# Pool makes a token tile's second norm as soon as its statistics are there, and more key tiles go to P·V as f16 products

## The chip, the cores and the metric

The kernel runs on one core of a Trainium2 chip. The metric is device time in microseconds (us): the median over executions of the program. The engines are named as in the profile: PE is the matrix engine (PEld its weight loads), DVE the vector engine, ACT the scalar engine, POOL the GpSimd engine, SP the engine whose queue issues most DMAs. Each engine works off its own instructions in the order in which the program wrote them; an instruction that waits for data holds up everything behind it on its engine.

## The reference

One transformer block with modulated layer norms: 2048 tokens, width 512, 32 query heads of 16 that share one key head and one value head, and a bilinear GLU of width 1792. Cut to what is computed:

```python
mod = (silu(c) @ w_mod).reshape(1, 6, 1, -1)
sa, ca, ga, sb, cb, gb = (mod[:, i] for i in range(6))
h = layernorm(x) * (1 + ca) + sa
q = (h @ wq).reshape(B, S, 32, 16).transpose(0, 2, 1, 3)
p = softmax(einsum("bhqd,bkd->bhqk", q, h @ wk) * 16 ** -0.5)
o = einsum("bhqk,bkd->bhqd", p, h @ wv)
x = x + ga * (o.transpose(0, 2, 1, 3).reshape(B, S, 512) @ wo)
h = layernorm(x) * (1 + cb) + sb
x = x + gb * (((h @ w_gate) * (h @ w_up)) @ w_down)
```

## The kernel before

**Units, blocks and turns.** The attention runs in 32 units (numbered 0 to 31). Four units in a row, with the same 256 queries and eight heads each, make a block; "a block's second unit" is unit 1, 5, 9, 13, 17, 21, 25 or 29. A unit goes over 16 key tiles of 128 keys, one in each turn, so there are 512 turns. In a turn PE makes four score tiles of 128 keys x 512 (`sc`), ACT makes their exponentials P (L690), PE finds running maxima for the unit after next (`mx`, L611, which DVE reduces, L615), and at the turn's end PE multiplies the exponentials of the turn before by the values (`pv`, L724), summed over the unit's key tiles in one PSUM bank. In the places between, PE does half matmuls of the side work (L520): the query projection, the output projection `wo` of the last block, gate and up (`wg`, `wu`), and down (`wd`). The order is written out by hand; nothing moves an instruction at run time.

Turns go in pairs: in the pair's first turn the exponentials of one row half are made for both key tiles, in the second those of the other half. So an even key tile's P is whole in the middle of the next turn, an odd one's at the end of its own.

**P·V in f32 and in f16.** Most key tiles go into P·V as f32: four matmuls with a 32-column output each (eight in the trace, as one f32 product shows as two). For a few key tiles, listed in `F16_AT` by the unit's place in its block and from unit `F16_FROM` on, P is written to one of two sets of places, Pool splits each of its four parts j = 0 to 3 into a high and a low f16 half (`p_split`, two instructions each, L696 and L697, both seen as `glu<-glu`), and PE makes three f16 products of four matmuls: high times value-high, high times value-low, low times value-high. The low halves are needed by the last four matmuls alone.

```python
def p_split(v, j):
    t, h = p_sets[f16_set[v]]
    nc.gpsimd.tensor_scalar(h[:, j, 0], t[:, j], 1.0, 0.0, op0=OP.mult, op1=OP.add)
    nc.gpsimd.tensor_tensor(h[:, j, 1], t[:, j], h[:, j, 0], op=OP.subtract)
```

An f16 tile's products are late by one f16 tile: they stand in the P·V place of the next f16 tile (`pv_place`), which is at the end of the turn behind that tile's own. The four splits are written into Pool's order in the middle of turns `f16_split`: before, in the four turns after the tile's, except for the first tile of a block's second unit, whose splits stand in its turns 1, 1, 9 and 10 (`F16_LATE`).

**The rest of Pool's order.** In the same queue stand: the second half of the GLU product, two instructions per group of gate and up (L929, L930), which wait for DVE's `gf`; `mult` of `normalise` (L765, L767, L768: the unit's attention output times the reciprocal sums, `M` below), at the end of turn 10 of the next unit; and the norm of the token tiles. After a block, `wo_work(sb)` adds the output projection for the block's two tiles of 128 tokens. At a tile's end DVE adds it to x; by timers that count half turns, DVE makes the statistics (3 and 4 half turns later, `spread` and `aggr`), and six small Pool instructions make the reciprocal deviation (L221 to L226). `nrm` then makes the norm: subtract and scale (L829 on Pool in blocks 2 to 5; elsewhere ACT, L831, which needs two more small Pool instructions, L823 and L824, for its bias), times and plus the modulation (L835, L836), and two f16 halves (L838, L839). Before, both tiles' norms wait for the second tile: they are written 4 and 9 half turns after its end. In blocks 1 to 6 (`by_dma`) a DMA transposes the result, and two half turns after that gate and up may start. Blocks are numbered from 0; all this falls in the second unit of the next block (block 3 in unit 17, block 6 in unit 29).

Of the kernel before, what the change touches and what calls it, by code (L numbers as in the profile page):

```python
# [25 lines left out]
NC = KC  # L26
NU = NS * NC
KT = S // 128
# [20 lines left out]
M_STEP = 23  # L49
PAIRED = 14  # L50
Q_BURSTS = {26: 3, 27: 3, 28: 3, 29: 3}
F16_FROM = 9
F16_AT = ((0, 5, 10), (0, 10), (0, 5, 10), (0, 5, 10))
F16_LATE = {0: (1, 1, 9, 10)}
P_SHIFT = float(14 * np.log(2.0))

LOW = -3.0e38
# [12 lines left out]
def adaln_mqa_glu_kernel(ctx: ExitStack, tc: tile.TileContext, x_in, wq_in, wk_in, wv_in, wo_in,  # L70
# [82 lines left out]
    for i in range(3):  # L153
        t = consts.tile([128, 2, 2, ST], F16, name=f"sst{i}")
# [73 lines left out]
    def rstd_of(st, n):  # L228
        y = work.tile([128, 4], F32, name="ry", bufs=6)[:, :n]
        rstd_into(y, st[:, :, 1], n)  # L230
        return y
# [155 lines left out]
    nc.gpsimd.memset(tok, 0.0)  # L387
    kts16 = sorted({k for ks in F16_AT for k in ks})
    v16 = consts.tile([128, 2, len(kts16), 32], F16, name="v16")
# [266 lines left out]
    pd = {}  # L656
    f16s = [KT * u + k for u in range(F16_FROM, NU) for k in F16_AT[u % NC]]
    assert f16s[0] % KT == 0
    f16_set = {v: i % 2 for i, v in enumerate(f16s)}
    f16_before = dict(zip(f16s[1:], f16s))  # L660
    f16_split = {}
    for v in f16s:
        late = v % KT == 0 and v // KT % NC == 1
        for j in range(4):
            f16_split.setdefault(v + (F16_LATE[0][j] if late else j + 1), []).append((v, j))
    p_sets = []
    did_pv = {}

# [108 lines left out]
    def after(delay, f):  # L777
        if tick[0] is None:
            f()
        else:  # L780
            timers.setdefault(tick[0] + delay, []).append(f)
# [5 lines left out]
    def load_x(t):  # L787
        if t < KT - 2:
            x1s[t] = work.tile([128, D], F32, name="x1", tag="x1", bufs=6)
        else:  # L790
            x1s[t] = work.tile([128, D], F32, name="x1p", tag="P", bufs=8)
        nc.sync.dma_start(x1s[t], x_rows[t * 128:(t + 1) * 128, :])

    def wo_work(sb):
        on_pool = 2 <= sb < NS - 2
        by_dma = 0 < sb < NS - 1

        def op(t):
            def f(i):
                ch, term = divmod(i, 3)  # L800
                ol, wl = TERMS[term]
                return [(och[sb, ch][:, ol, t * 128:(t + 1) * 128], wo[:, wl, ch, :])]
            return f

        def fin(t):
            row = 2 * sb + t

            def f(p):
                x1 = x1s[row]
                nc.vector.scalar_tensor_tensor(x1, p, sca[:, 7:8], x1, op0=OP.mult, op1=OP.add)  # L810
                s2 = work.tile([128, 1, 2], F32, name="st2", bufs=5)
                bs = work.tile([128, 6], F32, name="bs", bufs=4)
                nb = work.tile([128, 2], F32, name="nb", bufs=4)
                yt = {}

                def spread():
                    nc.vector.bn_stats(bs, x1)

                def aggr():
                    nc.vector.bn_aggr(s2[:, 0, :], bs)  # L820
                    yt["y"] = rstd_of(s2, 1)
                    if not on_pool:
                        nc.gpsimd.tensor_tensor(nb[:, 0:1], s2[:, 0, 0:1], yt["y"], op=OP.mult)  # L823
                        nc.gpsimd.tensor_scalar(nb[:, 1:2], nb[:, 0:1], -1.0, 0.0, op0=OP.mult, op1=OP.add)  # L824

                def nrm():
                    n2 = work.tile([128, D], F32, name="n2", tag="n2", bufs=2)
                    if on_pool:
                        nc.gpsimd.tensor_scalar(n2, x1, s2[:, 0, 0:1], yt["y"], op0=OP.subtract, op1=OP.mult)  # L829
                    else:  # L830
                        nc.scalar.activation(n2, x1, AF.Identity, bias=nb[:, 1:2], scale=yt["y"])  # L831
                    n2s[row] = n2
                    if not by_dma:
                        return
                    nc.gpsimd.tensor_tensor(n2, n2, cbb, op=OP.mult)  # L835
                    nc.gpsimd.tensor_tensor(n2, n2, sbb, op=OP.add)  # L836
                    n16 = work.tile([128, 2, D], F16, name="n16", tag="gf", bufs=4)
                    nc.gpsimd.tensor_scalar(n16[:, 0, :], n2, 1.0, 0.0, op0=OP.mult, op1=OP.add)  # L838
                    nc.gpsimd.tensor_tensor(n16[:, 1, :], n2, n16[:, 0, :], op=OP.subtract)  # L839
                    after(TR_LAG + (3 if sb < 2 else 0), lambda: ln2_turn(sb, t, n16))  # L840

                after(3, spread)
                after(4, aggr)
                n2f[row] = nrm
                if t == 1:
                    late = 3 if sb < 2 else 0
                    for j in range(2):
                        after((4, 9)[j] + late, n2f[2 * sb + j])
                    if sb == 0:
                        after(TR_WAIT + late, lambda: turns.extend(ln2_work(sb)))  # L850
            return f

        return [Group(3 * KC, op(t), fin(t), lambda t=t: load_x(2 * sb + t)) for t in range(2)]
# [6 lines left out]
    def ln2_turn(sb, t, n16):  # L860
        to = h2s[sb].rearrange("p l k n -> p (l k) n")[:, :, t * 128:(t + 1) * 128]
        nc.sync.dma_start(to, n16.rearrange("p l d -> p (l d)"), transpose=True)
        if t == 1:
            after(H2_LAG, lambda: h2done.add(sb))

    def ln2_work(sb):
        st = {}

        def tr(i):
            def f():  # L870
                if not h2s:
                    h2T = big.tile([128, 2, 2, KC, ST], F16, name="h2T", tag="wq")
                    both = big.tile([128, 2 * KC * S], F16, name="glu", tag="big")
                    n = 2 * FT * ST
                    glus.append(both[:, :n].rearrange("p (h f t) -> p h f t", h=2, f=FT))
                    p_places(both[:, n:])
                    h2s.update({s: h2T[:, s % 2] for s in range(NS)})
                st["p"] = ps_hold("mx")
                for k in range(2):
                    for t in range(2):  # L880
                        c = k * ST + t * 128
                        nc.tensor.transpose(st["p"][:, c:c + 128],
                                            n2s[2 * sb + t][:, (2 * i + k) * 128:(2 * i + k + 1) * 128], ident)
            return f

        def ev(i):
            def f():
                hf = work.tile([128, 2, ST], F32, name="hf", tag="g", bufs=2)
                for k in range(2):
                    nc.scalar.activation(hf[:, k, :], st["p"][:, k * ST:(k + 1) * ST], AF.Identity,  # L890
                                         bias=hsc[:, 2 * i + k, 0:1], scale=hsc[:, 2 * i + k, 1:2])
                ps_give(st["p"])
                eng = nc.vector if sb == NS - 1 else nc.gpsimd
                h = h2s[sb][:, :, 2 * i:2 * i + 2, :]
                eng.tensor_scalar(h[:, 0], hf, 1.0, 0.0, op0=OP.mult, op1=OP.add)  # L895
                eng.tensor_tensor(h[:, 1], hf, h[:, 0], op=OP.subtract)
                if i == 1:
                    (after if sb == 0 else lambda d, f: f())(3, lambda: h2done.add(sb))
            return f

        return [(900, tr(i), ev(i)) for i in range(2)]
# [386 lines left out]
    nrm = []  # L1288
# [149 lines left out]
    nrm = normalise(NU - 1)  # L1438
# [34 lines left out]
```

## Time and profile before

| | us |
|---|---|
| median of 3 runs | 1674.84 (1674.62 to 1675.54) |
| profiled execution, its own time | 1674.18 |
| its span in the trace | 1672.3 |
| PE busy | 1629.1 (97%) |
| DVE busy | 1401.4 (84%) |
| ACT busy | 1221.9 (73%) |
| POOL busy | 1004.5 (60%) |

The profile's page gives the busy time of each engine, the chain of work that ended last, and groups of instructions with mean durations and the idle time ahead of them. Below are also used: the waits of one engine by what ended them, the timeline of one engine (start, duration, instruction, and in brackets the idle time before it with what ended it), and windows, which give busy time and PE's granted clock (1.00 is full speed) between two moments. In the trace one turn takes about 2.85 us and one unit about 45.5 us.

### The profile page before, as it was taken

What the parts mean: (1) busy time and instruction counts of PE and PEld (TensorE: products, weight loads), DVE (VectorE), ACT (ScalarE), POOL (GpSimd) and SP (SyncE); (2) the same over time, 40 slices, a digit from 0 to 9 for tenths busy, and PEclk for the clock granted to TensorE, in tenths of its full rate; (3) what the DMA queues carried; (4) which work ended last, traced back from release to release, by engine and by line L of the source; (5) the groups of instructions that cost most, each with busy time, mean ns of one, the idle gap of its engine ahead of it and who ended that gap; (6) DMA issues with size and microseconds to landing.
All of it is one profiled execution on the core that took longest, in us unless ns stands there. A gap on an engine that the chain in (4) does not pass through costs nothing.

```text
span 1672.3 us, 41157 instructions
## 1 busy us (share of the span) xinstructions
PE 1629.1 (97%) x15881; PEld 752.0 (45%) x15881; DVE 1401.4 (84%) x2433; ACT 1221.9 (73%) x2428; POOL 1004.5 (60%) x1372
## 2 busy tenths in 40 slices
PE   9999999999999999999998999899998999999999
PEld 4333333355433554345532454434544345454776
DVE  8999999899998999999997999799997999890211
ACT  6688888888777887778876787677876777687310
POOL 6856637875847665756656565754647556655422
PEclk9999999999999999999999999999999999999999
DMA  7213213332311000100010001100001001100100
GB/s 264 89 55 102 92 56 113 104 120 80 89 44 30 20 18 28 35 26 20 19 38 24 25 19 30 25 25 26 20 27 29 23 20 30 32 15 21 33 13 14
DMA packets 78996, 79.14 MB, mean 47 GB/s; under 512 B 30408, under 2 KB 59340, under 8 KB 78800
## 3 DMA queue, kind: packets, MB, share of 16 engines
q1 hardware_dynamic: 77744, 76.46, 14.4%
q8 instruction: 124, 2.03, 0.5%
q14 instruction: 72, 0.59, 0.1%
q10 hardware_dynamic: 1056, 0.07, 0.0%
HBM read 56.04 MB, written 17.05 MB: 44 GB/s over the span
## 4 chain that ended last, share of the span: by engine, by line
PE 86%; POOL 6%; DVE 4%; ACT 2%; issue 1%; DMA 0%; SPq 0%; POOLq 0%; ACTq 0%; DVEq 0%
PE side L520 39%; PE pv L724 27%; PE sc L684 8%; PE mx L611 8%; DVE mpart L615 3%; PE sc L682 3%; ACT P L690 1%; POOL n L829 1%; POOL glu L697 1%; POOL n L836 1%; POOL n L835 1%; POOL n L839 1%; PE part L291 0%; DMA wmA<-in_w_mod_dram 0%; PE mxt L639 0%
## 5 line engine op out<-in xcount | busy, mean ns | idle before, releaser
L615 DVE TENSOR_REDUCE mpart<-mx 128x1 f32<-128x512 f32 x2016 | 1273.1, 684 | 118.5 <-PE mx L611 110.3
L690 ACT ACTIVATE P<-sc 128x512 f32<-128x512 f32 x1796 | 969.5, 599 | 247.7 <-PE sc L684 202.4
L611 PE MATMUL mx<-kst,sst 48*128 48x512 f16 x2032 | 633.0, 379 | 1.7 <-DVE mpart L615 0.6
L684 PE MATMUL sc<-sst,kst 51*128 51x512 f16 x1792 | 601.3, 381 | 0.7 <-ACT P L690 0.3
L520 PE MATMUL side<-h2T,wg 64*128 64x256 f16 (+1 forms) x2396 | 544.3, 272 | 0.5 <-POOL h2T L895 0.3
L520 PE MATMUL side<-h2T,wu 64*128 64x256 f16 (+1 forms) x2396 | 541.7, 271 | 0.0
L724 PE MATMUL pv<-P,vst 128*32 128x512 f32 x3592 | 480.1, 607 | 0.7
L520 PEld LDWEIGHTS <-wg 64*128 64x128 f16 (+1 forms) x2396 | 227.3, 95 | 222.7 <-ACT P L690 156.6
L697 POOL TENSOR_TENSOR glu<-glu 128x512 f16<-128x512 f32 x252 | 291.8, 1158 | 21.1
L520 PE MATMUL side<-wd,glu 64*128 64x512 f16 (+1 forms) x1172 | 273.1, 379 | 0.2 <-ACT P L690 0.2
L520 PEld LDWEIGHTS <-wu 64*128 64x128 f16 (+1 forms) x2396 | 227.8, 95 | 40.2 <-issue 2.8
L696 POOL TENSOR_SCALAR glu<-glu 128x512 f16<-128x512 f32 x252 | 155.6, 618 | 98.0 <-ACT glu L690 67.8
L611 PEld LDWEIGHTS <-sst 48*128 48x128 f16 x2064 | 192.0, 95 | 32.0 <-issue 14.7
L929 POOL TENSOR_SCALAR glu<-gf 128x256 f16<-128x256 f32 x112 | 45.8, 408 | 264.1 <-DVE gf L928 262.2
L684 PEld LDWEIGHTS <-kst 51*128 51x128 f16 x1792 | 163.7, 95 | 63.9 <-issue 51.1
L520 PEld LDWEIGHTS <-glu 64*128 64x128 f16 (+1 forms) x1172 | 99.2, 95 | 188.7 <-ACT P L690 66.6
L690 ACT ACTIVATE glu<-sc 128x512 f32<-128x512 f32 x252 | 139.1, 596 | 60.3 <-PE sc L684 57.2
L724 PEld LDWEIGHTS pv<-P,vst 128*32 128x32 f32 x3592 | 71.1, 108 | 142.2 <-issue 132.5
L928 DVE TENSOR_TENSOR gf<-side,g 128x256 f32<-128x256 f32 x112 | 46.7, 417 | 79.5 <-ACT g L926 69.8
L682 PE MATMUL sc<-sst,kst 51*128 51x256 f16 x512 | 97.1, 269 | 0.0
L520 PE MATMUL side<-h,wq 64*128 64x512 f16 (+1 forms) x372 | 95.5, 378 | 0.4 <-ACT P L690 0.4
L926 ACT ACTIVATE g<-side 128x256 f32<-128x256 f32 x112 | 42.3, 379 | 66.1 <-PE side L520 65.7
(248 smaller groups left out, 1147.6 us busy)
## 6 DMA issues: line engine op xcount, KB each, us to landing
pd<-ev SPq DMA_DIRECT2D x32, 256.0 KB
kwb<-in_B_w_gate_dram SPq DMA_DIRECT2D x32, 224.0 KB
kwb<-in_B_w_up_dram SPq DMA_DIRECT2D x32, 224.0 KB
sst<-qd SPq DMA_DIRECT2D x180, 32.0 KB
qd<-q SPq DMA_DIRECT2D x16, 256.0 KB
oc<-pd SPq DMA_DIRECT2D x64, 64.0 KB
rr<-ri SPq DMA_DIRECT2D x64, 64.0 KB
x<-in_A_x_dram SPq DMA_DIRECT2D x14, 256.0 KB
```

The lines of the kernel that those rows point to most:

```text
L520: return nc.tensor.matmul(self.p[:, c * w:(c + 1) * w], left[rows], right[rows], start=start and c == 0, stop=stop and c == len(terms) - 1)
L611: nc.tensor.matmul(m, s[64 * a:64 * a + 48, t // 2, p, t % 2 * 128:(t % 2 + 1) * 128], w[64 * a:64 * a + 48, :], start=(i == 0), stop=(i = ...
L615: nc.vector.tensor_reduce(part, m, axis=AX.X, op=OP.max)
L682: nc.tensor.matmul(t[:, c * ST:(c + 1) * ST], keys, s[64 * a:64 * a + 51, c, p, :], start=True, stop=True)
L684: nc.tensor.matmul(t.rearrange("k (c n) -> k c n", c=2), keys, s[64 * a:64 * a + 51, :, p, :], start=True, stop=True)
L690: ex = nc.scalar.activation(ptl[u, kt, p, a], t, AF.Exp)
L696: nc.gpsimd.tensor_scalar(h[:, j, 0], t[:, j], 1.0, 0.0, op0=OP.mult, op1=OP.add)
L697: nc.gpsimd.tensor_tensor(h[:, j, 1], t[:, j], h[:, j, 0], op=OP.subtract)
L724: nc.tensor.matmul(pvb[u][32 * j:32 * j + 32, :], vt, ps[j], start=start and n == 0, stop=stop and n == len(terms) - 1)
L926: nc.scalar.activation(g, p[:, 0:ST], AF.Copy, scale=2.0 ** -45)
L928: nc.vector.tensor_tensor(gf, p[:, ST:2 * ST], g, op=OP.mult)
L929: nc.gpsimd.tensor_scalar(glu()[:, 0, f, :], gf, 1.0, 0.0, op0=OP.mult, op1=OP.add)
```

## The change

Two things change. The norm of a token tile is written one half turn after its own statistics (`after(5, nrm)`; 8 in block 1) and no longer waits for the block's second tile. And the f16 tiles go from three per unit (two in a block's second unit) from unit 9 on to four per unit (again two in the second) from unit 10 on: 78 tiles where there were 63. The splits of every tile now stand in the four turns after its own, with j = 2 one turn earlier where the next tile follows after three or four turns; `F16_LATE` is gone.

```diff
-F16_FROM = 9
-F16_AT = ((0, 5, 10), (0, 10), (0, 5, 10), (0, 5, 10))
-F16_LATE = {0: (1, 1, 9, 10)}
+F16_FROM = 10
+F16_AT = ((0, 4, 8, 11), (0, 9), (0, 4, 8, 11), (0, 4, 8, 11))
...
-    for v in f16s:
-        late = v % KT == 0 and v // KT % NC == 1
+    for v, n in zip(f16s, f16s[1:] + [KT * NU]):
         for j in range(4):
-            f16_split.setdefault(v + (F16_LATE[0][j] if late else j + 1), []).append((v, j))
+            f16_split.setdefault(min(v + j + 1, n - (j == 2)), []).append((v, j))
...
                 n2f[row] = nrm
-                if t == 1:
+                if by_dma:
+                    after(5 + (3 if sb < 2 else 0), nrm)
+                elif t == 1:
                     late = 3 if sb < 2 else 0
                     for j in range(2):
                         after((4, 9)[j] + late, n2f[2 * sb + j])
```

From L52 on, lines move up by one or two (L696, L697 become L694, L695; L829 becomes L827; L765 becomes L763). The number and place of PE's side matmuls are the same in every turn from unit 10 on.

**Pool in a block's second unit (unit 17).** The splits are the pairs `glu<-glu`; `n_18284` and `n_18437` before, `n_18250` after are the norms of the first or second token tile. Before, the third split, the second norm, the fourth split and the first instruction of `M`:

```order
L696 TENSOR_SCALAR glu<-glu 128x512
L697 TENSOR_TENSOR glu<-glu 128x512
L829 TENSOR_SCALAR n_18437<-x_18021,st_18194,ry 128x512
L835 TENSOR_TENSOR n_18437<-n_18437,cbb 128x512
L836 TENSOR_TENSOR n_18437<-n_18437,sbb 128x512
L838 TENSOR_SCALAR n_18441<-n_18437 128x512
L839 TENSOR_TENSOR n_18441<-n_18437,n_18441 128x512
L696 TENSOR_SCALAR glu<-glu 128x512
L697 TENSOR_TENSOR glu<-glu 128x512
L765 TENSOR_TENSOR oc<-oc,rr 128x256
```

After, the end of the first tile's statistics, the fourth split, the first tile's norm, and the start of the second tile's statistics:

```order
L225 TENSOR_TENSOR ry<-ry,rt 128x1
L694 TENSOR_SCALAR glu<-glu 128x512
L695 TENSOR_TENSOR glu<-glu 128x512
L827 TENSOR_SCALAR n_18250<-x_17978,st_18137,ry 128x512
L833 TENSOR_TENSOR n_18250<-n_18250,cbb 128x512
L834 TENSOR_TENSOR n_18250<-n_18250,sbb 128x512
L836 TENSOR_SCALAR n_18254<-n_18250 128x512
L837 TENSOR_TENSOR n_18254<-n_18250,n_18254 128x512
L220 TENSOR_SCALAR rv<-st_18300 128x1
```

All four splits of the unit's first f16 tile now stand ahead of both norms.

**Pool in turns 9 to 11 of unit 12 (a block's first unit).** Before, the GLU halves of turn 9, then `M`, then the split of turn 11:

```order
L929 TENSOR_SCALAR glu<-gf 128x256
L930 TENSOR_TENSOR glu<-gf,glu 128x256
L765 TENSOR_TENSOR oc<-oc,rr 128x256
L767 TENSOR_SCALAR och<-oc 128x256
L768 TENSOR_TENSOR och<-oc,och 128x256
L696 TENSOR_SCALAR glu<-glu 128x512
L697 TENSOR_TENSOR glu<-glu 128x512
```

After, the GLU halves of turn 9, the splits j = 1 and j = 2 of key tile 8 in turn 10, `M`, and in turn 11 the split j = 3:

```order
L929 TENSOR_SCALAR glu<-gf 128x256
L930 TENSOR_TENSOR glu<-gf,glu 128x256
L694 TENSOR_SCALAR glu<-glu 128x512
L695 TENSOR_TENSOR glu<-glu 128x512
L694 TENSOR_SCALAR glu<-glu 128x512
L695 TENSOR_TENSOR glu<-glu 128x512
L763 TENSOR_TENSOR oc<-oc,rr 128x256
L765 TENSOR_SCALAR och<-oc 128x256
L766 TENSOR_TENSOR och<-oc,och 128x256
L694 TENSOR_SCALAR glu<-glu 128x512
L695 TENSOR_TENSOR glu<-glu 128x512
```

Two splits now stand between the GLU halves and `M`, and the split behind `M` is the fourth one of key tile 8, whose products stand at the end of turn 12.

**ACT in unit 29 (the second unit of a block whose norms ACT makes).** The norm of the first token tile is `n2_24904` before and `n2_24946` after; `P` are exponentials, `ev` copies out the last unit's P·V. Before, the norm stands 19 exponentials behind `ev`; the rows around it:

```order
L690 ACTIVATE P_24870<-sc_24871 128x512
L690 ACTIVATE P_24881<-sc_24882 128x512
L690 ACTIVATE P_24887<-sc_24888 128x512
L831 ACTIVATE n2_24904<-x1_24499,nb_24660,ry_24737 128x512
L690 ACTIVATE P_24930<-sc_24931 128x512
```

After, from `ev` on:

```order
L733 ACTIVATE ev_24834<-pv_23953 128x512
L688 ACTIVATE P_24844<-sc_24845 128x512
L688 ACTIVATE P_24853<-sc_24854 128x512
L688 ACTIVATE P_24858<-sc_24859 128x512
L688 ACTIVATE P_24878<-sc_24879 128x512
L688 ACTIVATE P_24893<-sc_24894 128x512
L688 ACTIVATE P_24902<-sc_24903 128x512
L688 ACTIVATE P_24907<-sc_24908 128x512
L688 ACTIVATE P_24938<-sc_24939 128x512
L829 ACTIVATE n2_24946<-x1_24672,nb_24833,ry_24912 128x512
L688 ACTIVATE P_24954<-sc_24955 128x512
```

It stands eight exponentials behind `ev`, at the start of turn 5, half a turn behind the statistics.

## The prediction

> **What bounds the kernel now.** I read the page first, then PE's waits, then windows over single units, then the timelines of PE and POOL at the longest waits. Each unit number is the kernel's; Tn is the start of P·V in turn n of the unit spoken of.
>
> ```profile
> PE 1629.1 (97%) x15881; PEld 752.0 (45%) x15881; DVE 1401.4 (84%) x2433; ACT 1221.9 (73%) x2428; POOL 1004.5 (60%) x1372
> PE 86%; POOL 6%; DVE 4%; ACT 2%; issue 1%; DMA 0%; SPq 0%; POOLq 0%; ACTq 0%; DVEq 0%
> ```
>
> PE bounds it; POOL holds 6% of the chain that ended last. Of PE's waits one kind stands out (us in total, times, longest):
>
> ```profile
> PE pv L724 <- POOL glu L696: 24.1, 5, 7.0
> PE pv L724 <- POOL glu L697: 1.8, 5, 0.6
> ```
>
> These are f16 P·V products that wait for a split. They lie in units 9, 17, 21, 25 and 29. Windows over unit 13 (a block's second unit without such a wait) and the last four:
>
> ```profile
> 667.10:712.90 45.80, 45.80 (x399) 14.44 (x391) 42.55 (x73) 34.97 (x70) 34.92 (x42) 1.00 0.13 35
> 849.40:904.80 55.40, 48.23 (x426) 16.96 (x418) 43.52 (x75) 35.29 (x70) 35.36 (x47) 0.94 0.09 24
> 1040.90:1096.30 55.40, 48.35 (x482) 21.42 (x474) 44.28 (x78) 36.17 (x73) 37.48 (x51) 0.94 0.09 24
> 1232.10:1287.60 55.50, 48.45 (x523) 24.51 (x515) 44.49 (x79) 36.65 (x74) 34.63 (x48) 0.94 0.09 25
> 1423.60:1476.80 53.20, 49.58 (x523) 24.87 (x515) 44.20 (x77) 37.88 (x75) 31.13 (x50) 0.94 0.09 25
> ```
>
> Over unit 13's 45.8 they are longer by 9.6, 9.6, 9.7 and 7.4, in all 36.3 us. That is more than the waits, because PE comes back with a slow clock (eighth column, granted clock). PE and POOL in unit 17:
>
> ```profile
> 874.88 0.40 PE L724 MATMUL pv<-glu,v 128*32 128x512 f16 x3
> 882.25 1.04 PE L724 MATMUL pv<-glu,v 128*32 128x512 f16 x8 [6.97 <-POOL glu L696]
> ```
> ```profile
> 874.91 2.07 POOL L829 TENSOR_SCALAR n<-x,st,ry 128x512 f32<-128x512 f32 x1
> ...
> 881.58 0.62 POOL L696 TENSOR_SCALAR glu<-glu 128x512 f16<-128x512 f32 x1
> 882.28 1.16 POOL L697 TENSOR_TENSOR glu<-glu 128x512 f16<-128x512 f32 x1
> ```
>
> The first three of twelve matmuls run; the fourth needs the split j = 3, which stands behind the whole second norm (874.91 to 881.58).
>
> **First part: the norms and the four early splits.** In units 17, 21, 25 and 29 all four splits now stand ahead of both norms, in turns 1 to 4, and their products in turn 10, so the waits go. Ahead of the fourth split only three splits and the first tile's statistics stand; it is written in turn 4, and its product comes at the end of turn 10, six turns of some 2.85 or 17 us later. POOL spends no more on the norms (6.7 each, 874.91 to 881.58); it makes them earlier. Gain 36.3. Unit 9 has no f16 tile any more; its wait goes as well:
>
> ```profile
> 507.80 0.40 PE L724 MATMUL pv<-glu,v 128*32 128x512 f16 x3
> 508.85 0.62 PE L724 MATMUL pv<-glu,v 128*32 128x512 f16 x8 [0.64 <-POOL glu L696]
> 510.08 0.38 PE L724 MATMUL pv<-glu,v 128*32 128x512 f16 x1 [0.62 <-POOL glu L697]
> 510.39 0.39 PE L520 MATMUL side<-wd,glu 64*128 64x512 f16 x1
> ```
>
> From its start to the next matmul it takes 2.59; undisturbed (rows below) 0.76. Gain 1.8. The transposing DMA of a norm on SP follows its norm and comes earlier with it; gate and up start no earlier, since PE's side work keeps its places, so I cost that at nothing (without the cover of SP's other DMAs, one transposition).
>
> **Second part: 15 more f16 tiles on PE.** From unit 12:
>
> ```profile
> 640.73 1.06 PE L724 MATMUL pv<-P,vst 128*32 128x512 f32 x8
> 641.73 0.28 PE L520 MATMUL side<-h2T,wg 64*128 64x256 f16 x1
> ...
> 643.57 1.07 PE L724 MATMUL pv<-P,vst 128*32 128x512 f32 x8
> ...
> 646.42 0.83 PE L724 MATMUL pv<-glu,v 128*32 128x512 f16 x12
> 647.18 0.28 PE L520 MATMUL side<-h2T,wg 64*128 64x256 f16 x1
> ...
> 649.09 1.07 PE L724 MATMUL pv<-P,vst 128*32 128x512 f32 x8
> ```
>
> Start to the next matmul: 1.00 for f32, 0.76 for f16, so 0.24 a tile: 15 x 0.24 = 3.6 gained. A turn takes 2.84 after an f32 block and 2.60 after an f16 one.
>
> **Third part: what they cost on POOL.** 15 tiles are 60 splits more. POOL in unit 12:
>
> ```profile
> 642.42 0.41 POOL L929 TENSOR_SCALAR glu<-gf 128x256 f16<-128x256 f32 x1 [1.48 <-DVE gf L928]
> 643.53 0.73 POOL L765 TENSOR_TENSOR oc<-oc,rr 128x256 f32<-128x256 f32 x1
> 645.48 0.62 POOL L696 TENSOR_SCALAR glu<-glu 128x512 f16<-128x512 f32 x1
> 646.18 1.16 POOL L697 TENSOR_TENSOR glu<-glu 128x512 f16<-128x512 f32 x1
> 647.42 0.62 POOL L696 TENSOR_SCALAR glu<-glu 128x512 f16<-128x512 f32 x1
> ```
>
> So a split takes 1.94 of POOL (645.48 to 647.42), M 1.95, the GLU halves 1.11, and these start 1.69 after the P·V of the turn in which they are written (642.42 against 640.73). 60 x 1.94 = 116 us of POOL, hidden on average: a unit then has 16 splits, five GLU pairs and one M, 31.0 + 5.6 + 2.0 = 39 of some 45. It is not hidden at key tile 8, whose products moved from the sixth turn behind the tile to the fourth (turn 12) and whose fourth split stands behind M.
>
> - Units 12, 16, 20, 24, 28, which have GLU halves in turn 9: these start at T9 + 1.69, split j = 1 at 2.80, j = 2 at 4.74, M at 6.68, j = 3 at 8.63, and its second instruction ends at 8.63 + 0.70 + 1.16 = 10.49. P·V of turn 12 starts at T9 + 8.36 (640.73 to 649.09, which also holds one f16 block). Its three groups of four matmuls start 0.22 to 0.23 apart (an estimate from the 0.76), so the twelfth is due at 8.36 + 0.45 = 8.81 and starts at 10.54: 1.73 lost. Five units: 8.7.
> - Units 11, 15, 19, 23, 30, with GLU halves in turns 7 and 10: in T7's time 1.69 halves, 2.80 tile 4's j = 3, then tile 8's j = 0, 1, 2 at 4.74, 6.68, 8.62, the next halves at 10.56, M at 11.67, j = 3 at 13.62, done at 15.48. P·V of turn 12: four turns of 2.84 and one of 2.60, 13.96; the twelfth matmul due at 14.41: 1.1 lost. Five units: 5.5.
> - Units 10 and 31, with GLU halves in turn 8: in T8's time 1.69 halves, then tile 8's j = 0 at 2.80, and two splits, M and j = 3 behind it, done at 12.43; the twelfth matmul due at 3 x 2.84 + 2.60 + 0.45 = 11.57: 0.9 lost each, 1.8.
> - Units 14, 18, 22, 26, 27 have no halves near: j = 3 is done some 2 us before.
>
> Together 16.0, PE's new wait. From below it is 0 if M or the halves come early enough; from above, the rival on the clock. I take the count, since every duration in it has a row. The other new tiles keep about 1 us (tile 0 of the first list, tile 4 of the second) or more.
>
> **Fourth part: ACT in unit 29.** Its norms stay on ACT, whose bias needs POOL's eight small instructions, and the norm now stands half a turn behind the statistics:
>
> ```profile
> 1428.73 0.23 POOL L221 TENSOR_SCALAR rv<-st 128x1 f32<-128x1 f32 x1 [7.72 <-DVE st L820]
> ...
> 1431.06 0.19 POOL L824 TENSOR_SCALAR nb<-nb 128x1 f32<-128x1 f32 x1
> ```
> ```profile
> 1427.50 2.17 ACT L690 ACTIVATE P<-sc 128x512 f32<-128x512 f32 x4 [0.73 <-PE sc L684]
> 1430.36 2.25 ACT L690 ACTIVATE P<-sc 128x512 f32<-128x512 f32 x4 [0.69 <-PE sc L684]
> ...
> 1437.59 0.81 ACT L831 ACTIVATE n<-x,nb,ry 128x512 f32<-128x512 f32 x1
> ```
>
> ACT is free at 1429.67, the bias is there at 1431.25; the norm holds ACT for 0.71 (1437.59 to the next at 1438.30), so turn 5's exponentials start at 1431.96 where they started at 1430.36. Behind them waits the P·V of key tile 4, which needs the first two of them: 1.3 late. The second tile repeats it in turn 8, where no P·V needs the exponentials at once: between 0 and 1.3; I take 1.0. Lost 2.3; from below 0, from above 2.9 (1.6 + 1.3). In unit 9 the norms come three half turns later still, and ACT need not wait. More f16 tiles also add 15 one-element ACT instructions; they lie beside PE.
>
> **Sum.** 1674.2 (profiled execution) - 36.3 - 1.8 - 3.6 + 16.0 + 2.3 = 1650.8; the median of the runs is 0.7 above the profiled one, so 1651.5. That is 1.4% less; 0.2% (3.3 us) is about what can be told from no change.
>
> **Rivals.**
>
> - POOL keeps up and the new waits don't come, because PE's turns in these units are longer than I took: 1651.5 - 16.0 = 1635.5. Against it: the order puts M between the splits, and 2.84 and 2.60 have rows.
> - The new waits slow PE's clock. The rows that show when it falls (PE's timeline, then windows around the idle times of 1.68, of 0.64 and 0.62, and after unit 29's):
>
> ```profile
> 123.82 0.43 PE L1043 MATMUL mx<-kwb,onec 128*32 128x128 f32 x8 [1.68 <-POOL kwb L1033]
> ```
> ```profile
> 120.00:129.00 9.00, 7.23 (x52) 1.88 (x49) 5.63 (x10) 4.97 (x11) 8.03 (x9) 0.81 0.55 173
> 505.00:512.00 7.00, 5.74 (x54) 1.89 (x52) 4.81 (x9) 4.74 (x11) 6.58 (x9) 1.00 0.01 2
> 1453.30:1460.20 6.90, 6.29 (x39) 2.73 (x40) 2.58 (x4) 2.28 (x4) 6.48 (x10) 0.51 0.18 40
> ```
>
>   An idle time of 1.68 was followed by half clock (0.81 over 9 us: 3.4 us at half); idle times of 0.64 and 0.62 in unit 9 were not (1.00); unit 29's wait was followed by 6.9 at 0.51, which costs up to 3.4. My new waits are two short ones of about half a us each, like unit 9's. If each of the 12 tripped the clock at 3.4, it would be 41 more: 1692.5, slower. It decides from 1.9 a unit on (23 over 12). If four of them trip, 1665.
>   The Trainium skill's page "TensorE: Matmul & The Clock Gate", Part 1, says that the clock halves after at least one idle window of about 3.4 us; by that no wait forecast here trips it, this rival has no chance and the sum stays. The 1.68 row disagrees, so I leave the rival a chance.
> - The norms move but the old waits stay in part, as POOL reaches the four splits late: half of 36.3 back gives 1669.6. Against it: between the norms and turn 10 lie no more than a split and the halves.
> - DVE takes over in the shorter turns, and the 0.24 is lost on all tiles: 1655, inside the range. Four reduces in a turn at 1273.1 / 2016 = 0.63 are 2.53, just under 2.60:
>
> ```profile
> L615 DVE TENSOR_REDUCE mpart<-mx 128x1 f32<-128x512 f32 x2016 | 1273.1, 684 | 118.5 <-PE mx L611 110.3
> ```
>
> **Chances and range.** As summed 0.72 (own range 1645 to 1658), no new waits 0.1, clock 0.09 (0.03 of it slower than before), old waits in part 0.05, DVE 0.04. Faster by over 0.2%: 0.95; within: 0.02; slower: 0.03. The range goes down to 1639 (most of the new waits gone) and up to 1663 (a few trips).
>
> **What will show it.** PE's waits lose the 7 us ones and gain some 20 short ones on the splits in turn 12, with about 0.5 or less on L694 and on L695 each; windows over the second units are near 46 at clock 1.00; POOL rises by 60 x (0.62 + 1.16) = 107 to about 1111 busy; f16 P·V counts 936, f32 3472; in unit 29 ACT waits for `nb`. Wrong if the clock falls at turn 12, or if a split is late where I count 1 us to spare.

## The result and the profile after

The changed kernel takes 1654.09 us (median of 4 runs, 1654.0 to 1657.02) against 1675.19 of the kernel before on the same chip: ratio 0.9878, 95% interval 0.9861 to 0.9895. The forecast was 1651.5, range 1639 to 1663. Medians below are of executions in the chip's fast state; one execution of the first experiment, 1804.35 us at a mean granted clock of 0.85, was in the slow state and is not in them.

The page of the changed kernel, engines and the chain that ended last:

```profile
PE 1620.8 (98%) x15941; PEld 751.6 (45%) x15941; DVE 1401.7 (85%) x2433; ACT 1221.5 (74%) x2443; POOL 1110.7 (67%) x1496
PE 90%; POOL 3%; DVE 2%; ACT 2%; issue 1%; DMA 1%; SPq 0%; POOLq 0%; ACTq 0%; DVEq 0%
```

POOL is busy 106 us longer, PE 8 us less; POOL's part of the chain fell from 6% to 3%. PE's waits in the changed kernel (us in total, times, longest):

```profile
PE pv L722 <- POOL glu L695: 6.2, 12, 0.6
PE mx L610 <- ACT P L688: 4.2, 5, 1.4
...
PE pv L722 <- POOL glu L694: 1.9, 5, 0.4
...
PE side L519 <- POOL h2T L895: 1.4, 1, 1.4
...
PE mx L610 <- DMA sst<-qd: 1.1, 1, 1.1
```

The 7 us waits are gone. In their place stand 17 short ones on the splits, in twelve units, and three kinds that the kernel before hardly had: on ACT's exponentials, on `h2T`, and on the loads of `sst`. Windows over unit 13 and units 17, 21, 25, 29 of the changed kernel (length, then busy time of PE, PEld, DVE, ACT and POOL, granted clock, DMA share, GB/s):

```profile
670.40:717.80 47.40, 46.26 (x399) 14.47 (x391) 42.74 (x73) 35.12 (x70) 35.05 (x42) 1.00 0.13 34
855.60:901.50 45.90, 45.90 (x426) 17.07 (x418) 43.55 (x75) 35.30 (x70) 33.71 (x45) 1.00 0.15 29
1039.30:1085.30 46.00, 46.00 (x482) 20.64 (x474) 44.21 (x77) 36.03 (x72) 35.73 (x49) 1.00 0.11 29
1223.20:1269.30 46.10, 46.10 (x523) 23.76 (x515) 44.36 (x78) 36.47 (x73) 32.83 (x46) 1.00 0.11 30
1406.00:1455.40 49.40, 46.63 (x523) 23.81 (x515) 44.84 (x78) 37.89 (x75) 29.47 (x48) 1.00 0.12 27
```

Three of the four long units fell to 46 at full clock. Unit 29 kept 3.4 us too many, and unit 13 became longer by 1.5 (the windows' edges are rounded to 0.1).

The new wait in turn 12, as forecast, in unit 12 (PE's timeline, then POOL's):

```profile
651.12 0.40 PE L722 MATMUL pv<-glu,v 128*32 128x512 f16 x3
651.91 0.61 PE L722 MATMUL pv<-glu,v 128*32 128x512 f16 x8 [0.39 <-POOL glu L694]
653.15 0.38 PE L722 MATMUL pv<-glu,v 128*32 128x512 f16 x1 [0.63 <-POOL glu L695]
...
655.30 1.06 PE L722 MATMUL pv<-P,vst 128*32 128x512 f32 x8
```
```profile
649.30 0.72 POOL L763 TENSOR_TENSOR oc<-oc,rr 128x256 f32<-128x256 f32 x1
650.11 0.41 POOL L765 TENSOR_SCALAR och<-oc 128x256 f16<-128x256 f32 x1
650.60 0.67 POOL L766 TENSOR_TENSOR och<-oc,och 128x256 f16<-128x256 f32 x1
651.24 0.62 POOL L694 TENSOR_SCALAR glu<-glu 128x512 f16<-128x512 f32 x1
651.94 1.16 POOL L695 TENSOR_TENSOR glu<-glu 128x512 f16<-128x512 f32 x1
```

The fourth split starts when `M` ends, at 651.24, 0.12 after its products were due; PE waits for its first half and again for its second. The turn takes 4.18 (651.12 to 655.30) where one after an f16 block takes 2.61.

### The profile page after: what moved, and what is told of

The parts are those of the page before. It is cut to its first block, busy times and chain, and to the rows that moved or that the text cites. A ratio compares the mean times of both kernels' runs of the same rounds, so it can differ in the third digit from the quotient of the medians.

```text
span 1652.2 us, 41523 instructions
## 1 busy us (share of the span) xinstructions
PE 1620.8 (98%) x15941; PEld 751.6 (45%) x15941; DVE 1401.7 (85%) x2433; ACT 1221.5 (74%) x2443; POOL 1110.7 (67%) x1496
## 4 chain that ended last, share of the span: by engine, by line
PE 90%; POOL 3%; DVE 2%; ACT 2%; issue 1%; DMA 1%; SPq 0%; POOLq 0%; ACTq 0%; DVEq 0%
PE side L519 40%; PE pv L722 28%; PE mx L610 8%; PE sc L682 8%; PE sc L680 3%; ACT P L688 2%; DVE mpart L614 2%; POOL glu L695 1%; PE misc L179 1%; POOL glu L694 1%; PE sc L278 0%; PE pk L298 0%; PE part L290 0%; PE mxt L638 0%; PE sc L610 0%
## 5 line engine op out<-in xcount | busy, mean ns | idle before, releaser
L688 ACT ACTIVATE P<-sc 128x512 f32<-128x512 f32 x1736 | 938.0, 599 | 206.8 <-PE sc L682 163.9
L722 PE MATMUL pv<-P,vst 128*32 128x512 f32 x3472 | 462.2, 605 | 0.7
L695 POOL TENSOR_TENSOR glu<-glu 128x512 f16<-128x512 f32 x312 | 361.2, 1158 | 26.1
L694 POOL TENSOR_SCALAR glu<-glu 128x512 f16<-128x512 f32 x312 | 192.7, 618 | 95.5 <-ACT glu L688 60.2
L688 ACT ACTIVATE glu<-sc 128x512 f32<-128x512 f32 x312 | 172.8, 595 | 74.7 <-PE sc L682 73.3
L610 PEld LDWEIGHTS <-sst 48*128 48x128 f16 x2064 | 190.0, 94 | 35.3 <-issue 18.6
```

Of the source, the lines that this page charges most:

```text
L610: nc.tensor.matmul(m, s[64 * a:64 * a + 48, t // 2, p, t % 2 * 128:(t % 2 + 1) * 128], w[64 * a:64 * a + 48, :], start=(i == 0), stop=(i = ...
L688: ex = nc.scalar.activation(ptl[u, kt, p, a], t, AF.Exp)
L722: nc.tensor.matmul(pvb[u][32 * j:32 * j + 32, :], vt, ps[j], start=start and n == 0, stop=stop and n == len(terms) - 1)
```

## Experiments

The question was where the 21 us came from, and which part of the change gives something back. All kernels were compared with the kernel before on the same chip (1675.19 us for the first four experiments, 1673.59 for the others); the sums below use medians.

**One constant of the kernel before: the four splits in turns 1 to 4.**

```diff
-F16_LATE = {0: (1, 1, 9, 10)}
+F16_LATE = {0: (1, 2, 3, 4)}
```

> The kernel before with one constant changed: the four splits of the first f16 tile of a block's second unit stand in its turns 1, 2, 3, 4 instead of 1, 1, 9, 10. Norms and the 63 tiles stay. Theory (the gain comes from where those splits stand, not from the earlier norms): the waits of units 9, 17, 21, 25 and 29 go, as the fourth split then stands ahead of both norms in POOL's order; 1675.2 less about 35.3 and 1.8, so 1637 to 1639, faster than the changed kernel's 1654.1. Rival (POOL makes the norms too late unless they are moved): some of the 7 us waits stay, 1650 or more.

Measured: 1635.60 us (three executions, 1634.83 to 1639.46), ratio 0.9773 (0.9757 to 0.979): 1.4 below what the theory gave, and 18.5 us faster than the whole change. In its trace units 9, 17, 21, 25 and 29 lost 1.8, 9.7, 9.4, 9.3 and 6.9 us, together 37.1, which is the theory's 35.3 and 1.8. Windows over units 17 and 25, which took 55.4 and 55.5:

```profile
849.70:895.50 45.80, 45.80 (x426) 16.42 (x418) 43.55 (x75) 35.27 (x71) 32.81 (x43) 1.00 0.11 30
1213.70:1259.80 46.10, 46.10 (x523) 23.76 (x515) 44.22 (x79) 36.48 (x74) 32.90 (x46) 1.00 0.11 30
```

So the gain needs neither the norms' move nor the additional tiles: it is enough that the last two of the four splits stand ahead of the norms in POOL's order.

**The norms' move alone on the kernel before.**

```diff
-                if t == 1:
+                if by_dma:
+                    after(5 + (3 if sb < 2 else 0), nrm)
+                elif t == 1:
```

> The kernel before with the earlier norms alone; splits in turns 1, 1, 9, 10 and 63 tiles stay. Theory: in POOL's order the second norm now stands ahead of the split of turn 9, so the fourth split follows the norm, the GLU halves and the third split instead of splitting around the norm; by the counted durations 1.5 us are left of each 8 us wait in units 17, 21, 25, the clock does not fall, and ACT's wait in unit 29 (3.2) and the late loads in unit 13 (1.5) come: 1675.2 - 35.3 + 4.5 + 3.2 + 1.5, so about 1648 to 1650. Rival (the norm's move does nothing, all of the gain is the splits'): 1675.

Measured: 1651.45 us, ratio 0.9861 (0.9845 to 0.9878); 1.5 above the upper end of what the theory gave. Windows over units 9 and 17, then the P·V block on PE, the waiting row of unit 9 and all of unit 17's:

```profile
478.70:534.70 56.00, 51.76 (x420) 15.93 (x414) 46.42 (x80) 38.55 (x76) 31.04 (x47) 0.94 0.14 33
853.80:901.40 47.60, 46.30 (x426) 16.54 (x418) 43.51 (x75) 35.20 (x71) 35.50 (x47) 1.00 0.11 28
```
```profile
510.77 0.70 PE L724 MATMUL pv<-glu,v 128*32 128x512 f16 x8 [3.17 <-POOL glu L696]
...
879.28 0.40 PE L724 MATMUL pv<-glu,v 128*32 128x512 f16 x3
880.36 0.61 PE L724 MATMUL pv<-glu,v 128*32 128x512 f16 x8 [0.68 <-POOL glu L696]
881.60 0.38 PE L724 MATMUL pv<-glu,v 128*32 128x512 f16 x1 [0.62 <-POOL glu L697]
```

In unit 17 the 7 us wait shrinks to two of 0.68 and 0.62, as counted. The miss is in unit 9, which I had not counted: its wait grows to 3.17, the clock falls (0.94 over the unit), and the unit takes 56.0 instead of 50.7. That the total came so near is partly luck: unit 13 kept its 45.8, so the 1.5 expected for its late loads did not come, and units 0 and 1, which the edit does not touch, took 1.0 less in its trace than in that of the kernel before. The norms' move, too, takes most of the old wait away; with the splits in turns 1 to 4 there is nothing left for it to take.

**The changed kernel with the norms put back.**

```diff
-                if by_dma:
-                    after(5 + (3 if sb < 2 else 0), nrm)
-                elif t == 1:
+                if t == 1:
```

> The changed kernel with the norms put back to 4 and 9 half turns after the second tile; 78 f16 tiles and their split turns stay. Theory: the norms' move is worth nothing here and costs ACT's wait in unit 29 (3.2) and the late loads of unit 13 (1.5): 1654.1 - 4.7, so 1649 to 1650, and the two turns of 4.5 us in unit 29 and the turn of 4.3 us in unit 13 are gone. Rival (the earlier norms carry the gain): the 7 us waits come back, 1675 or more.

Measured: 1648.88 us, ratio 0.9846 (0.9832 to 0.9861): 5.2 faster than with the move. The 7 us waits did not come back. Windows over units 13 and 29:

```profile
667.20:713.00 45.80, 45.80 (x399) 14.44 (x391) 42.55 (x72) 34.93 (x70) 34.91 (x42) 1.00 0.13 35
1403.00:1449.60 46.60, 46.37 (x523) 23.84 (x515) 44.42 (x78) 37.79 (x75) 29.35 (x48) 1.00 0.11 29
```

Unit 13 is back from 47.4 to 45.8 and unit 29 from 49.4 to 46.6. Once the splits stand early, the norms' move costs more than it gives. Unit 17 took 47.0 here, 1.1 more than with the move, with a wait of 0.78 for `sst`, and unit 25 took 0.6 more; that is what the move gains. The move first acts in unit 9, and from there to the end of unit 31 the two traces differ by 3.0. The rest lies ahead of it, 1.6 of it in units 0 and 1, where the clock fell once more in the changed kernel's trace; that part is chance.

**The fourth split ahead of M.**

```diff
-            f16_split.setdefault(min(v + j + 1, n - (j == 2)), []).append((v, j))
+            f16_split.setdefault(min(v + j + 1, n - (j == 2 or n - v == 3)), []).append((v, j))
```

> The changed kernel with key tile 8's fourth split written in turn 10, ahead of the normalising multiplications M, instead of in turn 11 behind them; nothing else moves. Theory (the new wait in turn 12 is the fourth split behind M): M's 1.94 us leave the chain, so the waits of 0.9 and 1.6 us go in all units but unit 10, where M stands in turn 9 (0.8 stays): 1654.1 - 13, so 1640 to 1642, turn 12 back to 2.6 us. Rival (POOL is short of time as a whole, the place in its order does not matter): the wait only moves, 1650 or more.

Measured: 1640.84 us, ratio 0.9799 (0.9784 to 0.9813): 13.2 less than the changed kernel. Windows over units 11 and 12, which took 46.0 and 46.9 in the changed kernel:

```profile
576.60:621.80 45.20, 45.20 (x552) 25.72 (x545) 42.61 (x73) 36.76 (x76) 36.11 (x47) 1.00 0.06 19
621.80:667.20 45.40, 45.32 (x487) 21.25 (x486) 43.12 (x75) 36.41 (x75) 34.15 (x48) 1.00 0.10 29
```

POOL does the same work (34 of 45 us) in another order, and the waits are gone: it was the order, not a lack of POOL time. Unit 10, where M stands in turn 9, kept its wait as expected (48.6).

**ACT's norms in unit 29 one and a half turns later.**

```diff
-                    after(5 + (3 if sb < 2 else 0), nrm)
+                    after(5 if on_pool else 8, nrm)
```

> The changed kernel with the two norms of unit 29, which ACT makes, written 8 half turns after a tile's end instead of 5. Theory (ACT stood idle for POOL's bias with the exponentials behind it): the two turns of 4.5 us in unit 29 fall to 2.9, the unit from 49.4 to 46.2 us; 1654.1 - 3.2, so about 1651. Rival (the norm's own time on ACT, or the transposing DMA, makes them long): the turns stay long or others take their place, 1654.

Measured: 1651.64 us, ratio 0.9867 (0.9853 to 0.9882). Against the changed kernel's 0.9878 that is within the interval; the trace tells it. ACT in unit 29 of the changed kernel and of this one:

```profile
1409.87 2.17 ACT L688 ACTIVATE P<-sc 128x512 f32<-128x512 f32 x4 [0.73 <-PE sc L682]
1413.65 0.81 ACT L829 ACTIVATE n<-x,nb,ry 128x512 f32<-128x512 f32 x1 [1.61 <-DVE mpart L614]
1414.37 2.18 ACT L688 ACTIVATE P<-sc 128x512 f32<-128x512 f32 x4
```
```profile
1414.46 1.57 ACT L688 ACTIVATE P<-sc 128x512 f32<-128x512 f32 x3 [0.72 <-PE sc L682]
1415.91 0.82 ACT L829 ACTIVATE n<-x,nb,ry 128x512 f32<-128x512 f32 x1
1416.61 0.61 ACT L688 ACTIVATE P<-sc 128x512 f32<-128x512 f32 x1
```

POOL's last instruction for the bias and PE's wait behind that norm, both in the changed kernel:

```profile
1413.43 0.19 POOL L822 TENSOR_SCALAR nb<-nb 128x1 f32<-128x1 f32 x1
...
1415.00 0.37 PE L610 MATMUL mx<-kst,sst 48*128 48x512 f16 x1 [1.37 <-ACT P L688]
```

There ACT stands idle for 1.61 ahead of the norm; the trace puts it down to DVE, but POOL's last instruction for the bias ended at 1413.62, just before. Later in the order, the norm starts without a wait. The unit's window fell from 49.4 to 47.1; I expected 46.2, so 0.9 of the loss stayed.

**The values' halves out of the way of `h2T`.** For five key tiles instead of three, POOL makes ten small instructions instead of six when the first `h2T` is due, in unit 5. Here they come 40 half turns later.

```diff
-        for i, k in enumerate(kts16):
-            ...
+        def values():
+            for i, k in enumerate(kts16):
+                ...
+        after(40, values)
```

> The changed kernel with the f16 halves of the values (ten POOL instructions for five key tiles, six for three before) written 40 half turns later, out of the way of the first splits of h2T in unit 5. Theory (the four instructions more delay h2T and with it gate and up): PE's wait for h2T in unit 5, 1.35 us and 0.33 before the change, goes or falls under 0.4, and unit 5 takes 47.3 us or less, not 48.3; the whole time about 1 us less, too little to be told in one run. Rival (unit 5 varies from run to run): 48.3 again.

Measured: 1651.45 us in a single run, which says little on 1 us. Windows over unit 5 in the changed kernel and in this one:

```profile
292.00:340.40 48.40, 46.06 (x410) 17.48 (x402) 42.48 (x73) 39.02 (x77) 42.83 (x71) 1.00 0.30 90
```
```profile
290.60:337.40 46.80, 45.82 (x410) 17.58 (x402) 42.32 (x72) 38.86 (x76) 40.75 (x61) 1.00 0.30 93
```

The unit loses 1.5 and PE no longer waits for `h2T`. It is no chance: the unit took 48.3 in every trace that made ten instructions there (the changed kernel, norms put back, fourth split early, ACT later), 47.3 in every one with six, and 46.8 again in the two kernels that follow.

**Together: 78 tiles, norms put back, fourth split ahead of M, values' halves later.**

> The changed kernel's 78 tiles with norms put back to 4 and 9 half turns, tile 8's fourth split ahead of M, and the values' halves later. By the terms measured so far: 1648.9 (norms back) - 13 (turn 12) - 1 (unit 5), so 1634 to 1636, below 1637.5, the best so far. If POOL's fuller queue makes new waits that the single experiments did not have: 1638 or more.

Measured: 1636.59 us, ratio 0.9779 (0.9764 to 0.9793). **The same with tiles at 0, 4, 8 and 12:**

> As the last, but with the f16 tiles at 0, 4, 8 and 12 instead of 0, 4, 8 and 11, so that tile 8's products come a turn later and its fourth split stands in turn 12. Theory (what counts is when the fourth split is due, by its place or by its distance): no waits on splits, also not unit 10's 0.8: 1633 to 1635. If the split of tile 12 in the next unit's turn 0 comes too late: waits at the next unit's turn 1, 1640 or more.

Measured: 1637.47 us, ratio 0.9782 (0.9766 to 0.9798). Both beat the two kernels of this study, but their ratios cannot be told from the 0.9773 of the one constant, and both lie above what was expected, by 0.6 and 2.5. In the second the waits moved: unit 31 is longer there than in any other trace (39.6), with 0.43 and 0.62 for its splits in the trace. In the first, unit 10's P·V wait stayed (0.41). Its units 17 and 25, to be set beside those of the first experiment:

```profile
848.70:895.40 46.70, 46.24 (x426) 17.08 (x418) 43.63 (x75) 35.34 (x70) 33.80 (x46) 1.00 0.11 28
1212.40:1258.90 46.50, 46.38 (x523) 23.80 (x515) 44.39 (x78) 36.54 (x73) 33.00 (x47) 1.00 0.13 29
```

From the end of unit 8 to the end of unit 31 this kernel takes 1043.2, the one constant 1043.6. By the forecast's price the 15 tiles give 3.6, so 3.2 of it is lost again: 0.9 and 0.4 in these two units (for `sst`, 0.46 on PE in unit 17), 0.9 in units 9 and 10, and less than half a us each elsewhere. Why unit 25 is longer, where PE's waits show nothing over 0.3, stays open.

## Why the prediction was right, point by point

- **The old waits (forecast -36.3).** Units 17, 21 and 25 lost 9.5, 9.4 and 9.4; unit 29 lost 3.8 net and, without its new wait on ACT of 3.2, 7.0: together 35.3. The step held; the place of the splits alone reproduces it.
- **Unit 9 (-1.8).** Units 9 and 10 together went from 96.3 to 95.8. The forecast for the two is -1.8 + 0.9 for unit 10's new wait + 0.2 for one f16 tile less, which is -0.7.
- **0.24 a tile (-3.6).** Units 14, 18, 22, 26 and 27, which have one tile more and no wait, became shorter by 1.1 in all: 0.22 a tile, or 3.5 for the 16 tiles more in units 11 to 31. So DVE did not take over.
- **New waits in turn 12 (+16.0).** They came in exactly the twelve units named. Turn 12 took 4.18 in units 12, 16, 20, 24 and 28, 1.57 over 2.61 (counted 1.73), and 0.85 to 0.94 over it in units 11, 15, 19, 23 and 30 (counted 1.1), 0.75 in unit 10 and 0.74 in 31 (counted 0.9): 13.9 in all. Part of the difference is that from a split to M it takes less than from one split to the next: 647.48 to 649.30 is 1.82, not 1.94.
- **ACT in unit 29 (+2.3).** 3.2: two turns of 4.52 and 4.51 where 2.93 was usual. Each tile costs 1.6, where I counted 1.3 and 1.0. I let PE wait at the P·V that needs the exponentials; it waits at a `mx` matmul (1.37 and 1.35), which takes its PSUM place from the same rotation as the score tiles. PE stops because the score tiles are not read in time, whether or not P·V needs the exponentials at once.
- **Costed at nothing, and wrong: the transposing DMAs on SP.** In unit 13 both norms come so early that their two transposes stand one behind the other in SP's queue, and the second waits for POOL's norm. SP's queue, changed kernel and norms put back:

```profile
677.54 15.64 SPq L862 DMA_TRANSPOSE h2T<-n  x2
...
696.11 2.75 SPq L575 DMA_DIRECT2D sst<-qd  x6
```
```profile
689.61 1.27 SPq L860 DMA_TRANSPOSE h2T<-n  x1
690.98 2.85 SPq L575 DMA_DIRECT2D sst<-qd  x6
```

  PE's wait in the changed kernel:

```profile
698.97 0.59 PE L610 MATMUL mx<-kst,sst 48*128 48x512 f16 x2 [1.14 <-DMA sst<-qd]
```

  SP is held for 15.6 us, the loads of `sst` behind the transposes issue 25.7 after the unit's start instead of 23.8 (the unit starts at 670.4 in the changed kernel, at 667.2 with the norms put back), and PE waits 1.14 for them. I named the cover, SP's other DMAs, and did not ask who waits behind a DMA that waits. The unit lost 1.5. It takes both parts of the change: with the norms' move alone SP is held for 10.15, the loads issue 22.1 after the unit's start, and the unit keeps its 45.8.
- **Not named: the ten small instructions in unit 5 (1.0 us).** They follow from the list of key tiles in `F16_AT`, three different ones before and five after, far from the lines that the diff touches. Another 1.1 us lie in units 6 and 7 (94.4 before, 95.5 after). In unit 7 ACT waits 1.09 for a load of `w_down`, 0.22 before the change, and PE then waits 0.80 for ACT's exponentials. The two units vary from 94.2 to 95.6 between the traces, so I do not put that down to the change.
- **The rival on the clock** did not come: no new wait halved it. Together (unit 10's 0.75 is in the -0.5 of units 9 and 10 already, so turn 12 counts 13.2) the terms give -35.3 - 0.5 - 3.5 + 13.2 + 3.2 + 1.5 + 1.0 + 1.1 = -19.3; the span fell by 20.1, so 0.8 stays without an account.

So the forecast was right by its main steps, the old waits and the new ones in turn 12. That it was only 2.6 us too low is partly luck: turn 12 cost 1.9 less than counted (13.2 against 15.1 without unit 10), which hides much of the 1.5, 1.0 and 1.1 that it left out and of the 1.0 and 0.9 by which the old waits and ACT came out worse. What it did not ask is whether the two parts of the change do the same thing twice: the place of the splits takes the old waits away alone, the norms' move takes most of them away alone, and on top of the splits it costs 3.0.

## What to carry to other kernels

When an engine waits for a queue that works in a fixed order, list what stands ahead of the late item and move that item first: here one constant was worth more than the whole change. Count a new item's latest start against the place where it is due, with the queue's own durations; twelve waits were placed that way before the kernel ran. For a step that is moved earlier, also ask what its waiting instructions hold up on each queue they stand in, DMA issue included.

## What the runs showed of the hardware that was not expected

The same idle time of PE halves the clock in one run and not in another. An idle time of 1.34 near 40 us is followed by full clock in the kernel before and by 3.4 us at half in the changed one; for the idle time of 1.68 (1.67) near 124 us it is the other way round. Windows around both, before and after:

```profile
38.00:50.00 12.00, 10.19 (x69) 6.22 (x70) 11.13 (x20) 11.30 (x24) 9.17 (x14) 1.00 0.55 232
120.00:133.00 13.00, 11.23 (x84) 2.93 (x79) 9.40 (x17) 8.32 (x17) 11.74 (x12) 0.87 0.39 124
```
```profile
38.00:50.00 12.00, 10.48 (x62) 6.36 (x59) 9.68 (x18) 10.20 (x21) 7.87 (x11) 0.86 0.58 243
120.00:133.00 13.00, 11.23 (x96) 3.45 (x88) 10.65 (x19) 9.70 (x20) 10.80 (x11) 1.00 0.40 124
```

The idle time of 2.06 near 54 us was followed by 6.8 us at half in all traces. Of the ten traces, the idle time of 1.34 was followed by half clock in five and that of 1.68 in three.

The stages of the granted clock show a grid. Every whole stage at half lasts 3.41 or 6.83 us, and within a trace they begin a whole number of 3.41 us apart: in the kernel before at 125.55 and at 879.89, which are 221 such steps. So the fall does not come at the wait, but at a moment of a grid that lies otherwise in each trace. In the five traces where the idle time of 1.34 was followed by half clock, it lay whole between two moments of the grid and ended 0.1 to 0.8 us before the second; in the other five it lay across one or began on one. For the idle time of 1.68 the place alone does not sort the traces: it lay whole between two moments in eight of them and was followed by half clock in three. What decides there stays open. A stage of 3.41 costs about 1.5 us (unit 1 took 43.90 in the kernel before, with the fall at 125.55, and 42.42 in the changed kernel, without one), so executions of one kernel differ by this much and more for reasons that no edit touches.

The Trainium skill's page "TensorE: Matmul & The Clock Gate", Part 1, says that the gate looks at a window that runs freely and is not reset by the kernel; the grid that lies otherwise in each trace agrees with that. The length needed does not agree: the page asks for about 3.4 us of idleness, and 1.34 was enough here.
